# Attention scores of a unit in four column tiles of one PSUM bank, in a decode kernel on one core

## The chip, the cores and the metric

The kernel runs on one core of a Trainium2 chip. The metric is the device time of one execution in microseconds. A profiled execution has a span (first to last recorded event) and a time of its own that is a little longer; both are given below. The engines are called PE (matrix products), DVE (vector), ACT (activation), POOL and SP; PEld is PE's loading of the stationary operand. All large loads are started from SP's queue, in the order of the program.

## What is computed

One decode step for a batch of 2 and a model width D of 448. `xn` is the layer norm of `x`. There are 16 query heads over 8 key/value heads of width 256, and the window is the last 2048 of 8192 cached positions. All inputs are bf16.

```python
xn = layernorm(A_x)                                  # (2, 1, 448)
q  = (xn @ wq).reshape(2, 1, 16, 256)                # two query heads share one kv head
k, v = k_cache[:, :, -2048:, :], v_cache[:, :, -2048:, :]
p  = softmax(q . k * 256 ** -0.5)                    # per head, over 2048 positions
s  = (p . v).reshape(2, 1, 4096) @ wo                # (2, 1, 448)
g  = silu(relu(xn @ w1) @ w2)                        # w1 448 x 1792, w2 1792 x 448
out = A_x + s * g
```

## The kernel before, in words

The work on keys and values is cut into four **units**, u = 0 to 3, each with four kv heads of one batch entry. A unit has one key load and one value load of 4 MB, each as 128 partitions of 64 positions x 256 numbers (`kv_src`). They go into three buffers `ub`, by the table `place` (L242). A load into a buffer in use waits for the last reader of what is in it (`freed`). SP issues the loads in program order, so a load that waits holds all later ones.

For each unit:

- `do_turn` (L251): four DVE transposes bring the keys, as 32-bit pairs, from `ub` into `kt`. They wait for the key load, and for the scores of the unit before, which read `kt`.
- `do_S` (L288): 36 PE matmuls write the scores into `sbk`, 128 x 2048 f32: four with the mask `amask`, then 32 that stream 512 columns of `kt` each. Every matmul uses all 128 columns of the array (stationary `qz`, 128 x 128). `amask` adds a large negative number where a query head and a key row don't belong together.
- `do_chain` (L302): DVE takes the maximum of each row of `sbk` (L303); PE turns the 128 maxima into a row (L305), DVE reduces it (L307), PE spreads it back to partitions, DVE copies it to `bias` (L311), ACT computes the exponentials into `e_sb` with their sums (L312), and DVE transposes `e_sb` in 32 x 32 blocks into `pt` (L315).
- `do_sum` (L318): PE adds the sums over partitions, DVE takes the reciprocal into `rs` (L321).
- `do_PV` (L323): 32 matmuls with a stationary operand of 128 x 32 from `pt` and 512 columns of the values, in four column tiles of the array (`tile_position`, 32 columns each) into `obk`.
- `do_o` (L333): DVE scales `obk` into `o_sb` (L335), four small PE products turn it, DVE writes `at_exp` (L345).

Around them stand `do_q` (the projection to `q`, in column tiles too), `do_H` and `do_F` (the two products with `w1` and `w2`), and the product with `wo`. `w1` and `w2` are loaded into the buffer of `v2` and wait for `do_PV(2)`. Every engine runs its instructions in the order in which the calls from L385 on write them down; across engines there are only semaphores. That order is: turn 0, q, S 0, chain 0, sum 0, turn 1, S 1, chain 1, sum 1, PV 0, o 0, turn 2, S 2, chain 2, sum 2, PV 1, o 1, turn 3, S 3, PV 2, o 2, chain 3, sum 3, PV 3, o 3, H, F, product with `wo`. Nearly all matmuls are recorded under line 230 (the helper `mm`), so they are told apart by their tiles.

Of the kernel before, what the change touches and what calls it, by code (L numbers as in the profile page):

```python
# [74 lines left out]
def bass_recurrent_scan__sliding_block_cached__dense_activation_relu__decode_kernel(  # L75
# [22 lines left out]
    NU = 4  # L98
# [9 lines left out]
    with es:  # L108
# [19 lines left out]
        gsum = named("gsum", [128, 128], F32)  # L128
        amask = named("amask", [128, 128], BF)
        x_sb = named("x_sb", [128, D], BF)  # L130
# [6 lines left out]
        q_n = named("q_n", [128, 2048], BF)  # L137
        qz = named("qz", [128, NU * 8 * 128], BF)
        h_n = named("h_n", [128, FC], BF)
# [8 lines left out]
        bias = named("bias", [128, 1], F32)  # L148
        e_sb = named("e_sb", [128, NT * 32], BF)
        ssum = named("ssum", [128, 1], F32)  # L150
        rs = named("rs", [128, NU], F32)
        pt = [named(f"pt{i}", [128, NT * 32], BF) for i in range(2)]
        o_sb = named("o_sb", [128, 512], BF)
# [5 lines left out]
        kt = named("kt", [128, UW], BF)  # L159
        W2O = SLOTS * FC  # L160
        assert W2O + 14 * D <= UW

        sbk = psum("sbk", [128, 2048], F32)
        obk = psum("obk", [128, 512], F32)
# [30 lines left out]
        p_one = pr.op(POOL, lambda e: e.memset(one_f[:, :], 1.0), [p_idf])  # L195
        p_mr = pr.op(POOL, lambda e: e.memset(mrow[0:1, :], 0.0))
        p_am = pr.op(POOL, lambda e: e.memset(amask[:, :], -BIG))
        p_qz = pr.op(POOL, lambda e: e.memset(qz[:, :], 0.0))  # L198
# [20 lines left out]
        def fold_op(e):  # L219
            with nc.allow_low_precision("zeros and ones"):  # L220
                return e.tensor_reduce(out=fold[:, :], in_=view(ident, 0, [[1, 32], [32, 4]]), axis=AX.X, op=ALU.add)
        v_fold = pr.op(DVE, fold_op)
        v_gs = pr.op(DVE, lambda e: e.tensor_copy(
            view(gsum, 0, [[16, 8], [2, 8], [1, 2]]), view(fold, 0, [[0, 8], [1, 8], [0, 2]])), [v_fold])
        v_am = pr.op(DVE, lambda e: e.tensor_scalar(
            out=view(amask, 0, [[32, 4], [2, 4], [1, 2]]), in0=view(ident, 0, [[0, 4], [1, 4], [0, 2]]),
            scalar1=-1.0, scalar2=BIG, op0=ALU.add, op1=ALU.mult), [p_am, p_id])

# [31 lines left out]
        def do_q():  # L260
            deps = [d_wq, v_xr, st["obz"]]
            for s in range(SLOTS):
                for i in range(4):
                    lo = s * HC + i * 512
                    o = pr.op(PE, mm(obk[32 * i:32 * i + 4, :], xr[:, 4 * s:4 * s + 4], wqo[:, lo:lo + 512],
                                     s == 0, s == SLOTS - 1, tile_position=(0, 32 * i)), deps)
                    deps = []
            st["q_mm"] = o
            a_z0 = st["obz"]
            v = pr.op(ACTE, lambda e: e.activation(  # L270
                view(q_n, 0, [[256, 8], [32, 4], [1, 32]]), view(obk, 0, [[64, 8], [0, 4], [2, 32]]),
                ACT.Copy, scale=SCALE), [o, a_z0])
            v2 = pr.op(DVE, lambda e: e.tensor_scalar(  # L273
                out=view(q_n, 128, [[256, 8], [32, 4], [1, 32]]), in0=view(obk, 1, [[64, 8], [0, 4], [2, 32]]),
                scalar1=SCALE, scalar2=None, op0=ALU.mult), [v])
            deps = [v, v2, st["mbk"]]
            for ch in range(2):
                for wp in range(8):
                    o = pr.op(PE, mm(view(mbk, 32 * wp + ch, [[2, 16]]),
                                     view(q_n, 128 * (8 * ch + wp), [[1, 128]]),  # L280
                                     view(ident, 0, [[2, 2], [1, 2], [32, 4]]), True, True), deps)
                    deps = []
            for Q in range(4):
                st["q"] = st["mbk"] = pr.op(ACTE, lambda e, Q=Q: e.activation(  # L284
                    view(qz, 32 * Q, [[1024, NU], [128, 8], [1, 8]], n=32, p0=32 * Q),
                    view(mbk, 0, [[8, NU], [32, 8], [1, 8]], n=32, p0=32 * Q), ACT.Copy), [o, p_qz])

        def do_S(u):  # L288
            deps = [st["q"], st.get(("exp", u - 1)), v_am] + [st["turn", u, g] for g in range(4)]
            for g in range(4):  # L290
                o = pr.op(PE, mm(view(sbk, 512 * g, [[1, 512]]), amask[:, :], view(ident, 0, [[0, 128], [1, 4]]),
                                 True), deps)
                deps = []
            for wp in range(8):
                for g in range(4):
                    o = pr.op(PE, mm(view(sbk, 512 * g, [[1, 512]]),
                                     view(qz, 1024 * u + 128 * wp, [[1, 128]]),
                                     view(kt, g * UW // 4 + 64 * (wp // 2) + wp % 2, [[256, 16], [2, 32]]),
                                     False, wp == 7), deps)
            st["S", u] = o  # L300

        def do_chain(u):  # L302
# [4 lines left out]
            v = pr.op(DVE, lambda e: e.tensor_reduce(  # L307
                out=view(mrow, 0, [[32, 4], [1, 8]], n=1), in_=view(mbk, 0, [[0, 4], [1, 8], [32, 4]], n=1),
                axis=AX.X, op=ALU.max, negate=True), [m, p_mr])
            m = pr.op(PE, mm(mbk_ap(128, 1), mrow[0:1, :], one_f[0:1, :], True, True), [v, p_one])  # L310
            v = st["mbk"] = pr.op(DVE, lambda e: e.tensor_copy(bias[:, :], mbk_ap(128, 1)), [m])  # L311
            a = st["exp", u] = pr.op(ACTE, lambda e: e.activation(  # L312
                e_sb[:, :], sbk[:, :], ACT.Exp, bias=bias[:, 0:1], accum_out=ssum[:, 0:1]),
                [v, st.get(("pt", u - 1)), st.get(("gs", u - 1))])
            st["pt", u] = pr.op(DVE, lambda e: e.transpose(  # L315
                view(pt[u % 2], 0, [[64, NT // 2], [1, 2], [2, 32]]), e_sb[:, :]), [a, st.get(("PV", u - 2))])

# [5 lines left out]
        def do_PV(u):  # L323
            v, p = ub[place[f"v{u}"]], pt[u % 2]
            deps = [dma_of[f"v{u}"], st["pt", u], st.get(("osb", u - 1)), st["q"]]
            for k in range(NT // 2):
                g = k % 4
                o = pr.op(PE, mm(obk[32 * g:32 * g + 32, :], view(p, 64 * k, [[1, 32]]),
                                 v[:, 512 * k:512 * k + 512], k < 4, k >= 28, tile_position=(0, 32 * g)), deps)
                deps = []  # L330
            st["PV", u] = freed[f"v{u}"] = o

        def do_o(u):  # L333
# [5 lines left out]
            for dblk in range(2):  # L339
                for ts in range(2):  # L340
                    o = pr.op(PE, mm(mbk_ap(136 + 8 * dblk, 8), o_sb[:, 256 * ts + 128 * dblk:256 * ts + 128 * dblk + 128],
                                     view(fold, ts, [[2, 8]]), dblk == 0 and ts == 0, ts == 1), deps)
                    deps = []
# [5 lines left out]

        w12 = ub[place["v2"]]  # L350

        def do_H():
            for u in range(2):
                deps = [st["w1"], st.get("h_n"), st["fbz"]]
                for s in range(SLOTS):
                    lo = s * FC + u * (FC // 2)
                    o = pr.op(PE, mm(fbk[0:4, 0:FC // 2], xr[:, 4 * s:4 * s + 4], w12[:, lo:lo + FC // 2],
                                     s == 0, s == SLOTS - 1), deps)
                    deps = []
# [10 lines left out]
        def do_F():  # L370
            deps = [st["w2"], st["hT"], st["fbz"]]
            for f in range(14):
                for i in range(4):
                    lo = W2O + f * D + i * NCOL
                    o = pr.op(PE, mm(fbk[32 * i:32 * i + B, 0:NCOL], h_sb[:, 2 * f:2 * f + 2], w12[:, lo:lo + NCOL],
                                     f == 0, f == 13, tile_position=(0, 32 * i)), deps)
                    deps = []
# [13 lines left out]
        st["wbz"] = pr.op(ACTE, lambda e: e.memzero(wbk[:, :]))  # L391
        do_turn(0)
        do_q()
        do_S(0)
        do_chain(0)
        do_sum(0)
        load("k2")
        do_turn(1)
        load("v1")
        do_S(1)  # L400
        do_chain(1)
        do_sum(1)
        do_PV(0)
        do_o(0)
        load("k3")
        do_turn(2)
        load("v2")
        do_S(2)
        do_chain(2)
        do_sum(2)  # L410
        do_PV(1)
        do_o(1)
        load("v3")
        do_turn(3)
        do_S(3)
        do_PV(2)
        st["w1"] = pr.dma(SP, w12[:, 0:SLOTS * FC], w1_src, [freed["v2"]])
        st["w2"] = pr.dma(SP, w12[:, W2O:W2O + 14 * D].rearrange("p (hf f) -> p hf f", hf=2), w2_src, [freed["v2"]])
        d_wo = []
        j0 = 0  # L420
        for n in WO_PARTS:
            d_wo.append((j0, pr.dma(SP, wqo[:, j0 * D:(j0 + n) * D], wo_src[:, j0 * D:(j0 + n) * D], [st["q_mm"]])))
            j0 += n
        do_o(2)
        do_chain(3)
        do_sum(3)
        do_PV(3)
        do_o(3)
        for b in range(2):
# [3 lines left out]
                view(at2, b, [[2, 32]]), mbk_ap(256 + 32 * b, 32)), [m_at])  # L433
        do_H()
        do_F()
# [46 lines left out]
```

## Time and profile before

| what | value |
|---|---|
| median of 3 runs (lowest, highest) | 159.79 us (157.24, 160.32) |
| time of the profiled execution, and its span | 158.94 us, 157.5 us |
| busy PE / PEld / DVE / ACT | 71.7 / 30.1 / 70.2 / 15.2 us |
| moved by DMA | 44.19 MB, 281 GB/s over the span |
| start of S 0, S 1, S 2, S 3 | 29.69, 56.92, 87.25, 117.77 us |
| start of turn 0, 1, 2, 3 | 13.29, 48.01, 78.31, 108.83 us |

The time lies 1.44 us above the span; that is kept as it is when a sum is made. The starts, from the timeline, show the rhythm: from one unit's scores to the next unit's it takes 27.2, 30.3 and 30.5 us. Durations are of the one profiled execution; the three times beside it differ by up to 2%.

### The profile page before, as it was taken

The page shows a single profiled execution, that of the slowest core. Times are in us where ns is not written, and L with a number is a line of the kernel's source. Part 1 is how long each engine was busy: PE and PEld are TensorE (multiplying, and loading weights), DVE is VectorE, ACT ScalarE, POOL GpSimd, SP SyncE. Part 2 cuts the span into 40 slices and gives each one's busy share as a digit, 9 for nine tenths or more (in the row PEclk, how much of TensorE's full clock was granted, in tenths as well). Part 3 has the DMA queues.
Part 4 walks back from the last instruction along what each step waited for, and adds up shares of the span by engine and source line. Part 5 has one row for each costly group of instructions (what it writes and reads, how often), then busy time and mean ns, then how long its engine had stood idle before and what let it go on. Part 6 is the DMA issues. An engine that isn't in the chain of part 4 may idle for free.

```text
span 157.5 us, 1293 instructions
## 1 busy us (share of the span) xinstructions
PE 71.7 (46%) x566; PEld 30.1 (19%) x566; DVE 70.2 (45%) x68; ACT 15.2 (10%) x20; POOL 5.2 (3%) x13
## 2 busy tenths in 40 slices
PE   0000043599210059924600898173009991346872
PEld 0000010234010013402100233030003440222252
DVE  2916963000649940064499101565980008252224
ACT  3300002700050000004000000220000000500000
POOL 7500000000000000000000000000000000000000
PEclk9999999999965556996555579955555899557699
DMA  4998999999996049930299899103992006999700
GB/s 134 466 466 350 466 441 474 400 400 458 474 400 271 0 133 400 400 133 0 67 391 449 333 416 424 50 4 133 400 416 117 0 0 207 416 434 409 287 1 5
DMA packets 2473, 44.19 MB, mean 281 GB/s; under 512 B 290, under 2 KB 548, under 8 KB 932
## 3 DMA queue, kind: packets, MB, share of 16 engines
q1 hardware_dynamic: 2440, 44.11, 67.2%
q8 instruction: 4, 0.07, 0.2%
q10 hardware_dynamic: 28, 0.00, 0.0%
q14 instruction: 1, 0.01, 0.0%
HBM read 44.11 MB, written 0.00 MB: 280 GB/s over the span
## 4 chain that ended last, share of the span: by engine, by line
PE 44%; DVE 32%; DMA 13%; ACT 7%; issue 2%; SPq 0%; DVEq 0%
PE sbk L230 26%; DVE kt L256 17%; DMA wqo<-in_A_wq_dram 13%; PE obk L230 10%; DVE rm L303 6%; ACT e_sb L312 5%; PE fbk L230 4%; PE mbk L230 3%; DVE pt L315 3%; DVE o_sb L335 2%; ACT qz L284 1%; DVE h_n L360 1%; PE mbk L305 1%; DVE q_n L273 1%; DVE mrow L307 1%
## 5 line engine op out<-in xcount | busy, mean ns | idle before, releaser
L256 DVE STREAM_TRANSPOSE kt<-ub 128x2048 f32<-128x2048 f32 x16 | 35.5, 2278 | 4.9 <-DMA ub<-in_A_k_cache_dram 4.9
L230 PE MATMUL sbk<-kt,qz 128*128 128x512 bf16 x128 | 34.6, 434 | 0.0
L303 DVE TENSOR_REDUCE rm<-sbk 128x1 f32<-128x2048 f32 x4 | 9.2, 2289 | 33.4 <-PE sbk L230 33.4
L230 PE MATMUL sbk<-ident,amask 128*128 128x512 bf16 x16 | 7.6, 627 | 30.6 <-DVE kt L256 28.9
L230 PEld LDWEIGHTS sbk<-kt,qz 128*128 128x128 bf16 x128 | 14.0, 110 | 21.4 <-issue 10.4
L312 ACT ACTIVATE e_sb<-sbk,bias 128x2048 bf16<-128x2048 f32 x4 | 7.9, 1968 | 98.2 <-DVE bias L311 98.2
L315 DVE STREAM_TRANSPOSE pt<-e_sb 128x2048 bf16<-128x2048 bf16 x4 | 10.0, 2498 | 8.5 <-ACT e_sb L312 8.5
L230 PE MATMUL obk<-ub,pt 128*32 128x512 bf16 x128 | 12.7, 567 | 2.0 <-DVE rs L321 2.0
L335 DVE TENSOR_SCALAR o_sb<-obk,rs 128x512 bf16<-128x512 f32 x4 | 3.0, 751 | 19.4 <-PE obk L230 19.4
L230 PE MATMUL obk<-wqo,xr 128*4 128x512 bf16 x28 | 3.2, 625 | 14.3 <-DMA wqo<-in_A_wq_dram 14.3
L230 PEld LDWEIGHTS sbk<-ident,amask 128*128 128x128 bf16 x16 | 1.7, 131 | 33.1 <-DVE kt L256 29.2
L230 PE MATMUL mbk<-ssum,gsum 128*128 128x1 f32 x8 | 2.3, 362 | 9.4 <-ACT e_sb L312 9.4
L230 PEld LDWEIGHTS obk<-ub,pt 128*32 128x32 bf16 x128 | 4.2, 128 | 7.8 <-issue 7.1
L305 PE MATMUL mbk<-ident_f,rm 128*1 128x128 f32 x4 | 1.2, 296 | 9.7 <-DVE rm L303 9.7
L230 PE MATMUL fbk<-ub,xr 128*4 128x448 bf16 x14 | 4.2, 459 | 0.7 <-DVE h_n L360 0.7
L230 PEld LDWEIGHTS mbk<-ssum,gsum 128*128 128x128 f32 x8 | 2.0, 312 | 9.7 <-ACT e_sb L312 9.7
L230 PEld LDWEIGHTS obk<-wqo,xr 128*4 128x4 bf16 x28 | 0.8, 114 | 15.9 <-DMA wqo<-in_A_wq_dram 14.4
L230 PE MATMUL mbk<-ident,xg 2*128 2x2 bf16 x7 | 0.3, 163 | 7.2 <-DVE xg L207 7.2
L198 POOL MEMSET qz<- 128x4096 bf16 x1 | 3.5, 3507 | 0.0
L360 DVE TENSOR_SCALAR h_n<-fbk 4x448 bf16<-4x448 f32 x2 | 1.2, 612 | 4.1 <-PE fbk L230 4.1
L273 DVE TENSOR_SCALAR q_n<-obk 128x1024 bf16<-128x1024 f32 x1 | 1.2, 1225 | 3.9 <-ACT q_n L270 3.9
L270 ACT ACTIVATE q_n<-obk 128x1024 bf16<-128x1024 f32 x1 | 1.0, 1024 | 19.6 <-PE obk L230 19.6
(61 smaller groups left out, 34.6 us busy)
## 6 DMA issues: line engine op xcount, KB each, us to landing
ub<-in_A_k_cache_dram SPq DMA_DIRECT2D x4, 4096.0 KB, 21.0
ub<-in_A_v_cache_dram SPq DMA_DIRECT2D x4, 4096.0 KB, 13.6
wqo<-in_A_wq_dram SPq DMA_DIRECT2D x1, 3584.0 KB, 20.3
ub<-in_B_w_dram SPq DMA_DIRECT2D x2, 1568.0 KB, 8.3
wqo<-in_A_wo_dram SPq DMA_DIRECT2D x2, 1120.0 KB, 13.9
wqo<-in_A_wo_dram SPq DMA_DIRECT2D x1, 896.0 KB, 16.9
wqo<-in_A_wo_dram SPq DMA_DIRECT2D x2, 224.0 KB, 17.0
x_c<-in_A_x_dram ACTq DMA_DIRECT2D x2, 0.9 KB
```

Of the source, the lines that this page charges most:

```text
L198: p_qz = pr.op(POOL, lambda e: e.memset(qz[:, :], 0.0))
L230: return lambda e: e.matmul(out_ap, lhsT=lhsT, rhs=rhs, start=start, stop=stop, skip_group_check=True, **kw)
L256: st["turn", u, g] = pr.op(DVE, lambda e, lo=lo, hi=hi: e.transpose(k32[:, lo:hi], s32[:, lo:hi]), [dma_of[f"k{u}"], st.get(("S", u - 1))])
L273: v2 = pr.op(DVE, lambda e: e.tensor_scalar(out=view(q_n, 128, [[256, 8], [32, 4], [1, 32]]), in0=view(obk, 1, [[64, 8], [0, 4], [2, 32]]) ...
L284: st["q"] = st["mbk"] = pr.op(ACTE, lambda e, Q=Q: e.activation(view(qz, 32 * Q, [[1024, NU], [128, 8], [1, 8]], n=32, p0=32 * Q), view(mb ...
L303: v = pr.op(DVE, lambda e: e.tensor_reduce(out=rm[:, :], in_=sbk[:, :], axis=AX.X, op=ALU.max), [st["S", u]])
L305: m = pr.op(PE, lambda e: e.matmul(mbk_ap(0, 128, 1), lhsT=rm[:, :], rhs=ident_f[:, :], start=True, stop=True, is_transpose=True), [v, p_i ...
L307: v = pr.op(DVE, lambda e: e.tensor_reduce(out=view(mrow, 0, [[32, 4], [1, 8]], n=1), in_=view(mbk, 0, [[0, 4], [1, 8], [32, 4]], n=1), ax ...
L312: a = st["exp", u] = pr.op(ACTE, lambda e: e.activation(e_sb[:, :], sbk[:, :], ACT.Exp, bias=bias[:, 0:1], accum_out=ssum[:, 0:1]), [v, st ...
L315: st["pt", u] = pr.op(DVE, lambda e: e.transpose(view(pt[u % 2], 0, [[64, NT // 2], [1, 2], [2, 32]]), e_sb[:, :]), [a, st.get(("PV", u - ...
L335: st["osb", u] = pr.op(DVE, lambda e: e.tensor_scalar(out=o_sb[:, :], in0=obk[:, :], scalar1=rs[:, u:u + 1], scalar2=None, op0=ALU.mult), ...
L360: st["h_n"] = pr.op(DVE, lambda e, u=u: e.tensor_scalar(out=h_n[0:4, u * (FC // 2):(u + 1) * (FC // 2)], in0=fbk[0:4, 0:FC // 2], scalar1= ...
```

## The change

1. **Scores.** The four groups g of a unit no longer fill 2048 columns of `sbk`; each goes to 32 partitions of a `sbk` of 128 x 512, in its own column tile of PE. The stationary operand is 128 x 32 (`qz` and `amask` shrink to 32 columns). There are still 36 matmuls of 512 moving columns.
2. **Maximum, exponentials and transpose** run over 512 columns instead of 2048.
3. **P is turned and spread.** DVE transposes `e_sb` (512 wide) into a new `ptd`; 16 matmuls (32 columns of the identity as stationary, 128 moving columns, in four column tiles) spread it into a new PSUM tile `pbk`; ACT copies that to `pt`. `do_PV` takes 16 columns of `pt` as stationary operand instead of 32.
4. **Own buffers** `w1_sb` and `w2_sb`, so that their loads wait for no reader.
5. **Order.** PV 0 and o 0 stand between turn 1 and S 1; PV 1 directly behind S 2 and before chain 2; chain 3 and sum 3 before o 2; H between o 2 and PV 3. SP's order is k0, wq, k1, v0, k2, v1, k3, v2, w1, v3, w2, wo.

The diff, cut to its core:

```diff
-        qz = named("qz", [128, NU * 8 * 128], BF)
+        qz = named("qz", [128, NU * 8 * 32], BF)
+        fold8 = named("fold8", [128, 8], F32)
...
-        sbk = psum("sbk", [128, 2048], F32)
+        w1_sb = named("w1_sb", [128, SLOTS * FC], BF)
+        w2_sb = named("w2_sb", [128, 14 * D], BF)
+        sbk = psum("sbk", [128, 512], F32)
+        pbk = psum("pbk", [128, 512], F32)
...
         def do_S(u):
             deps = [st["q"], st.get(("exp", u - 1)), v_am] + [st["turn", u, g] for g in range(4)]
-            for g in range(4):
-                o = pr.op(PE, mm(view(sbk, 512 * g, [[1, 512]]), amask[:, :], view(ident, 0, [[0, 128], [1, 4]]),
-                                 True), deps)
-                deps = []
-            for wp in range(8):
+            for wp in range(-1, 8):
                 for g in range(4):
-                    o = pr.op(PE, mm(view(sbk, 512 * g, [[1, 512]]),
-                                     view(qz, 1024 * u + 128 * wp, [[1, 128]]),
-                                     view(kt, g * UW // 4 + 64 * (wp // 2) + wp % 2, [[256, 16], [2, 32]]),
-                                     False, wp == 7), deps)
+                    if wp < 0:
+                        lhsT, rhs = amask[:, :], view(ident, 0, [[0, 128], [1, 4]])
+                    else:
+                        lhsT = view(qz, 256 * u + 32 * wp, [[1, 32]])
+                        rhs = view(kt, g * UW // 4 + 64 * (wp // 2) + wp % 2, [[256, 16], [2, 32]])
+                    o = pr.op(PE, mm(sbk[32 * g:32 * g + 32, :], lhsT, rhs, wp < 0, wp == 7,
+                                     tile_position=(0, 32 * g)), deps)
+                    deps = []
...
-            st["pt", u] = pr.op(DVE, lambda e: e.transpose(
-                view(pt[u % 2], 0, [[64, NT // 2], [1, 2], [2, 32]]), e_sb[:, :]), [a, st.get(("PV", u - 2))])
+            t = st["ptd", u] = pr.op(DVE, lambda e: e.transpose(ptd[:, :], e_sb[:, :]), [a, st.get(("sp", u - 1))])
+            deps = [t, st.get(("pt", u - 1))]
+            for g in range(4):
+                for Q in range(4):
+                    o = pr.op(PE, mm(pbk[32 * Q:32 * Q + 32, 128 * g:128 * g + 128], ident[:, 32 * g:32 * g + 32],
+                                     view(ptd, 8 * Q, [[32, 16], [1, 8]]), g == 0, True,
+                                     tile_position=(0, 32 * Q)), deps)
+                    deps = []
+            st["sp", u] = o
+            st["pt", u] = pr.op(ACTE, lambda e: e.activation(pt[u % 2][:, :], pbk[:, :], ACT.Copy),
+                                [o, st.get(("PV", u - 2))])
...
         do_turn(0)
+        load("k2")
         do_q()
...
-        load("k2")
         do_turn(1)
         load("v1")
+        do_PV(0)
+        load("k3")
+        do_o(0)
         do_S(1)
         do_chain(1)
         do_sum(1)
-        do_PV(0)
-        do_o(0)
-        load("k3")
         do_turn(2)
         load("v2")
+        st["w1"] = pr.dma(SP, w1_sb[:, :], w1_src)
         do_S(2)
+        do_PV(1)
+        load("v3")
         do_chain(2)
         do_sum(2)
-        do_PV(1)
         do_o(1)
-        load("v3")
-        do_turn(3)
-        do_S(3)
-        do_PV(2)
-        st["w1"] = pr.dma(SP, w12[:, 0:SLOTS * FC], w1_src, [freed["v2"]])
-        st["w2"] = pr.dma(SP, w12[:, W2O:W2O + 14 * D].rearrange("p (hf f) -> p hf f", hf=2), w2_src, [freed["v2"]])
+        st["w2"] = pr.dma(SP, w2_sb[:, :].rearrange("p (hf f) -> p hf f", hf=2), w2_src)
...
-        do_o(2)
+        do_turn(3)
+        do_S(3)
+        do_PV(2)
         do_chain(3)
         do_sum(3)
+        do_o(2)
+        do_H()
         do_PV(3)
...
-        do_H()
         do_F()
```

More of the change, by code (lines that the diff above doesn't have):

```diff
@@ L128, in bass_recurrent_scan__sliding_block_cached__dense_activation_relu__decode_kernel @@
         gsum = named("gsum", [128, 128], F32)
-        amask = named("amask", [128, 128], BF)
+        amask = named("amask", [128, 32], BF)
         x_sb = named("x_sb", [128, D], BF)
@@ L148, in bass_recurrent_scan__sliding_block_cached__dense_activation_relu__decode_kernel @@
         bias = named("bias", [128, 1], F32)
-        e_sb = named("e_sb", [128, NT * 32], BF)
+        e_sb = named("e_sb", [128, 512], BF)
+        ptd = named("ptd", [128, 512], BF)
         ssum = named("ssum", [128, 1], F32)
         rs = named("rs", [128, NU], F32)
-        pt = [named(f"pt{i}", [128, NT * 32], BF) for i in range(2)]
+        pt = [named(f"pt{i}", [128, 512], BF) for i in range(2)]
         o_sb = named("o_sb", [128, 512], BF)
@@ L159, in bass_recurrent_scan__sliding_block_cached__dense_activation_relu__decode_kernel @@
         kt = named("kt", [128, UW], BF)
-        W2O = SLOTS * FC
-        assert W2O + 14 * D <= UW
-        sbk = psum("sbk", [128, 2048], F32)
+        w1_sb = named("w1_sb", [128, SLOTS * FC], BF)
+        w2_sb = named("w2_sb", [128, 14 * D], BF)
+        sbk = psum("sbk", [128, 512], F32)
+        pbk = psum("pbk", [128, 512], F32)
         obk = psum("obk", [128, 512], F32)
@@ L195, in bass_recurrent_scan__sliding_block_cached__dense_activation_relu__decode_kernel @@
         p_one = pr.op(POOL, lambda e: e.memset(one_f[:, :], 1.0), [p_idf])
-        p_mr = pr.op(POOL, lambda e: e.memset(mrow[0:1, :], 0.0))
-        p_am = pr.op(POOL, lambda e: e.memset(amask[:, :], -BIG))
         p_qz = pr.op(POOL, lambda e: e.memset(qz[:, :], 0.0))
@@ L222, in bass_recurrent_scan__sliding_block_cached__dense_activation_relu__decode_kernel @@
         v_fold = pr.op(DVE, fold_op)
+        v_fold8 = pr.op(DVE, lambda e: e.tensor_reduce(
+            out=fold8[:, :], in_=view(ident, 0, [[1, 8], [8, 16]]), axis=AX.X, op=ALU.add), [p_id])
         v_gs = pr.op(DVE, lambda e: e.tensor_copy(
-            view(gsum, 0, [[16, 8], [2, 8], [1, 2]]), view(fold, 0, [[0, 8], [1, 8], [0, 2]])), [v_fold])
+            view(gsum, 0, [[8, 16], [1, 8]]), view(fold8, 0, [[0, 16], [1, 8]])), [v_fold8])
         v_am = pr.op(DVE, lambda e: e.tensor_scalar(
-            out=view(amask, 0, [[32, 4], [2, 4], [1, 2]]), in0=view(ident, 0, [[0, 4], [1, 4], [0, 2]]),
-            scalar1=-1.0, scalar2=BIG, op0=ALU.add, op1=ALU.mult), [p_am, p_id])
+            out=view(amask, 0, [[8, 4], [2, 4], [1, 2]]), in0=view(ident, 0, [[0, 4], [1, 4], [0, 2]]),
+            scalar1=-1.0, scalar2=BIG, op0=ALU.add, op1=ALU.mult), [p_id])
         def mm(out_ap, lhsT, rhs, start, stop=False, **kw):
@@ L284, in do_q @@
                 st["q"] = st["mbk"] = pr.op(ACTE, lambda e, Q=Q: e.activation(
-                    view(qz, 32 * Q, [[1024, NU], [128, 8], [1, 8]], n=32, p0=32 * Q),
+                    view(qz, 8 * Q, [[256, NU], [32, 8], [1, 8]], n=32, p0=32 * Q),
                     view(mbk, 0, [[8, NU], [32, 8], [1, 8]], n=32, p0=32 * Q), ACT.Copy), [o, p_qz])
@@ L307, in do_chain @@
             v = pr.op(DVE, lambda e: e.tensor_reduce(
-                out=view(mrow, 0, [[32, 4], [1, 8]], n=1), in_=view(mbk, 0, [[0, 4], [1, 8], [32, 4]], n=1),
-                axis=AX.X, op=ALU.max, negate=True), [m, p_mr])
+                out=view(mrow, 0, [[8, 16], [1, 8]], n=1), in_=view(mbk, 0, [[0, 16], [1, 8], [8, 16]], n=1),
+                axis=AX.X, op=ALU.max, negate=True), [m])
             m = pr.op(PE, mm(mbk_ap(128, 1), mrow[0:1, :], one_f[0:1, :], True, True), [v, p_one])
@@ L313, in do_chain @@
                 e_sb[:, :], sbk[:, :], ACT.Exp, bias=bias[:, 0:1], accum_out=ssum[:, 0:1]),
-                [v, st.get(("pt", u - 1)), st.get(("gs", u - 1))])
-            st["pt", u] = pr.op(DVE, lambda e: e.transpose(
-                view(pt[u % 2], 0, [[64, NT // 2], [1, 2], [2, 32]]), e_sb[:, :]), [a, st.get(("PV", u - 2))])
+                [v, st.get(("ptd", u - 1)), st.get(("gs", u - 1))])
+            t = st["ptd", u] = pr.op(DVE, lambda e: e.transpose(ptd[:, :], e_sb[:, :]), [a, st.get(("sp", u - 1))])
[9 more added lines that the diff above has]
+                                [o, st.get(("PV", u - 2))])
         def do_sum(u):
@@ L327, in do_PV @@
                 g = k % 4
-                o = pr.op(PE, mm(obk[32 * g:32 * g + 32, :], view(p, 64 * k, [[1, 32]]),
+                o = pr.op(PE, mm(obk[32 * g:32 * g + 16, :], view(p, 16 * k, [[1, 16]]),
                                  v[:, 512 * k:512 * k + 512], k < 4, k >= 28, tile_position=(0, 32 * g)), deps)
@@ L341, in do_o @@
                     o = pr.op(PE, mm(mbk_ap(136 + 8 * dblk, 8), o_sb[:, 256 * ts + 128 * dblk:256 * ts + 128 * dblk + 128],
-                                     view(fold, ts, [[2, 8]]), dblk == 0 and ts == 0, ts == 1), deps)
+                                     fold[:, 8 * ts:8 * ts + 8], dblk == 0 and ts == 0, ts == 1), deps)
                     deps = []
@@ L348, in do_o @@
                 in1=view(qmask, 0, [[0, 8], [0, 2], [1, 4]]), op=ALU.mult), [o, v_qm])
-        w12 = ub[place["v2"]]
         def do_H():
@@ L356, in do_H @@
                     lo = s * FC + u * (FC // 2)
-                    o = pr.op(PE, mm(fbk[0:4, 0:FC // 2], xr[:, 4 * s:4 * s + 4], w12[:, lo:lo + FC // 2],
+                    o = pr.op(PE, mm(fbk[0:4, 0:FC // 2], xr[:, 4 * s:4 * s + 4], w1_sb[:, lo:lo + FC // 2],
                                      s == 0, s == SLOTS - 1), deps)
@@ L373, in do_F @@
                 for i in range(4):
-                    lo = W2O + f * D + i * NCOL
-                    o = pr.op(PE, mm(fbk[32 * i:32 * i + B, 0:NCOL], h_sb[:, 2 * f:2 * f + 2], w12[:, lo:lo + NCOL],
+                    lo = f * D + i * NCOL
+                    o = pr.op(PE, mm(fbk[32 * i:32 * i + B, 0:NCOL], h_sb[:, 2 * f:2 * f + 2], w2_sb[:, lo:lo + NCOL],
                                      f == 0, f == 13, tile_position=(0, 32 * i)), deps)
```

## The prediction, made before the changed kernel was run

> **What bounds the kernel now.** I read the chain that ended last first, because no engine is busy for even half of the span.
>
> ```profile
> PE 44%; DVE 32%; DMA 13%; ACT 7%; issue 2%; SPq 0%; DVEq 0%
> ```
>
> Of this, the 13% of DMA is one piece, the wait for wq up to 21.77 us. Behind it the chain, in order of time, goes through PE, DVE and ACT one after another. One period of it, unit 1 (start, duration, what):
>
> ```profile
> 48.09 8.79 DVE kt L256 x4
> 56.88 0.05 issue
> 56.92 10.23 PE sbk L230 x36
> 67.15 0.02 issue
> 67.18 2.30 DVE rm L303
> ...
> 70.77 2.07 ACT e_sb L312 x2
> 72.84 0.04 issue
> 72.89 0.59 PE mbk L230 x2
> 73.47 3.56 PE obk L230 x24
> 77.03 0.02 issue
> 77.06 0.76 DVE o_sb L335
> ```
>
> Nothing overlaps here: turn, scores, maximum, exponentials, values, output, and then the next turn. No load stands in the period. The loads have room:
>
> ```profile
> DMA  4998999999996049930299899103992006999700
> ```
>
> Each digit is a slice of 3.94 us. Up to slice 13 the loads are dense (they are started ahead), then they come in bursts with gaps, because each waits for a reader. So the kernel is bound by latency along three engines; shortening a piece of the chain shortens the span, until the loads are dense everywhere.
>
> The third view is the stretches of scores and values (window, its length, busy PE, PEld, DVE, ACT, POOL; then granted clock, DMA share, GB/s):
>
> ```profile
> 56.90:61.50 4.60, 4.58 (x11) 1.58 (x12) 0.00 (x0) 0.00 (x0) 0.00 (x0) 0.50 0.76 278
> 61.50:67.15 5.65, 5.64 (x26) 2.30 (x24) 0.00 (x0) 0.00 (x0) 0.00 (x0) 1.00 0.98 423
> 73.40:77.00 3.60, 3.60 (x33) 1.12 (x32) 2.03 (x2) 0.00 (x0) 0.00 (x0) 0.50 0.00 0
> 128.20:130.10 1.90, 1.90 (x33) 0.76 (x32) 0.00 (x0) 0.00 (x0) 0.00 (x0) 1.00 0.00 0
> ```
>
> Scores start at half clock, 11 matmuls in 4.6 us (427 ns each); then the clock is full and 24 weight loads follow in 5.10 us (213 ns each). The 32 matmuls of PV, of the same 512 columns but in four column tiles, take 3.6 us at half clock and 1.9 us at full: four run side by side (8 x 427 ns = 3.42 us, and 0.18 us of drain).
>
> **The parts, step by step.**
>
> *Scores, 36 matmuls in four column tiles.* From the PV row: 9 x 427 ns + 0.18 = 4.03 us, at half clock, since the faster stretch comes only after 4.6 to 5.1 us of work. Now 10.2 us: 6.2 us less per unit. No row shows a tiled matmul whose moving operand is read with a step, as `kt` is (every second bf16). Bounds: 4.03 us if the step costs nothing, as it does untiled (213 ns for 512 columns is the rate of PV too); 36 x 427 + 180 ns = 15.5 us if the tiles don't overlap and the clock stays at half. I take 4.03, because the step is free in the nearest row.
>
> The Trainium skill speaks more modestly here: "TensorE: Matmul & The Clock Gate", Part 3, gives 3.07 times for four row tiles and 2.38 for three column tiles of 512 columns, while PV's 32 x 427 ns = 13.7 us in 3.6 us is 3.8 times. At 3.07 a unit's scores would take 5.0 us, and the sum below would end 4 us later; I go by the row.
>
> *Maximum over 512.* Between L307 (128 numbers, 0.28) and L303 (2048, 2.29) a number costs 1.05 ns: 0.68 us, was 2.29. *Exponentials:* between L270 (1024, 1.02) and L312 (2048, 1.97) a column costs 0.92 ns: 0.55 us, 0.65 with the reading of the sums, was 2.07. *Transpose:* 2.46 x 512 / 2048 = 0.62, with some overhead 0.65 us, was 2.46; bounds 0.62 and 0.75 (L335, 512 wide).
>
> *Spread, new.* Four groups of four matmuls of 128 columns: 4 x 107 ns + 0.18 = 0.6 us. Lower bound 0.4 (full clock); upper bound 16 serial weight loads of 146 ns (the longest of PV's), 2.3 us. I take 0.6, as in PV such loads run under the matmuls. *Copy on ACT:* about 0.55 us (the three 512-wide fills of L389 to L391 take 0.53 to 0.57). The compiled list of the changed kernel has two activation-table loads, as before, so Copy between exponentials adds none. The copy runs beside the sum's matmuls (0.59) and is hidden for all units; without that cover it costs 0.55 each, at most, in unit 3 only.
>
> So from the end of the scores to the reciprocal, with the waits of 0.02 to 0.05 of the chain: 0.70 + 0.32 + 0.31 + 0.43 + 0.19 + 0.67 + 0.67 + 0.64 + 0.60 + 0.16, together with 0.02 ahead, **4.71 us** (before, 8.2). The turn of the next unit is behind the reciprocal on DVE and needs the scores' `kt`; it starts there.
>
> *Order, walked through:*
> - S 0 starts at 29.69 as now (wq's landing, do_q and its qz copies are of the same size; the smaller qz fill on POOL, 3.5 us before 6.2, was never late). S 0 ends 33.72, reciprocal 38.43, turn 1 (8.80) to 47.23. k1 is long there.
> - PV 0 runs under turn 1: v0 was issued at 2.78 and the longest landing takes 38.4, so 41.2, and 3.6 later is 44.8. But o 0 now stands on DVE behind turn 1 and on PE ahead of S 1: 0.79 + 0.33 = 1.12 on the path. S 1 48.35 to 52.38, reciprocal 57.09, turn 2 to 65.89.
> - S 2 65.94 to 69.97. PV 1 is ahead of the row turn L305 in PE's queue, so chain 2 waits: its maximum is ready at 70.7, PV 1 ends at 72.3 (0.6 to 1.1 us at half clock, the rest at full: 2.3). This costs 1.6 of the 3.56 that PV 1 now costs behind the exponentials. Then 3.99 to the reciprocal, 76.26, o 1 as now 1.34, turn 3 (8.85) 77.60 to 86.45.
> - S 3 to 90.53, PV 2 2.3 to 92.83, 3.99 to 96.82, o 2 1.12: 97.94.
> - H now sits between o 2 and PV 3 in PE's queue and holds it: 2.61 + 0.66 + 2.61 + 0.66 + 0.54 = 7.08 (the first seven took 1.57 at full clock; then 6.0). To 105.0. P of unit 3 is ready by 97, so PV 3 waits for H alone. PV 3 takes 1.9 or 3.6 by the clock; after some 5 us of products with gaps I take the middle, 2.7: 107.7.
> - o 3 and the two turns of `at`: 2.08 (143.60 to 145.68 now), 109.8; from F's start to the last sum 3.31 (152.15 to 155.46), 113.1; the output 2.04, span **115.1**. With 1.44: **116.6 us**. The median of the runs shown is 0.85 above the profiled time, within what the runs differ, so I add nothing.
>
> *The loads under it.* k2 ends in slice 12, near 49.6, as now. Then v1 (issued 47.2 behind turn 1) and k3 with it, v2 and w1 behind turn 2 (65.9), v3 behind PV 1 (72.3), w2 and wo behind it. At 420 GB/s a load of 4.19 MB takes 10.0: v1 59.6, k3 69.6, v2 79.6, w1 83.4, v3 93.4, w2 97.2, wo 105.9. Each is 8 us or more ahead of its reader (turn 3 at 77.6, PV 2 at 90.5, H at 97.9, PV 3 at 105, F at 109.8), wo about 5. So the loads are dense from 1 to 106 us and hidden, and little more could be won without them binding.
>
> **Rivals.**
> 1. *The loads bind.* For it: the dense queue above. k3 and v2 moved 8.39 MB from 77.05 to about 98.9 now, 384 GB/s with the start. At that rate the 27.9 MB behind v0 (41.2) end at 113.7; then the last products and sums, 0.9, and 2.04: 116.6, time 118.1. If v3 holds PV 3, to 122. Against it: slices at 449 and 474.
> 2. *Stepped reads at half rate in tiles.* Scores 0.43 + 8 x 854 ns + 0.18 = 7.4 us, 3.4 more, four times: 130. Against it: the untiled row.
> 3. *The tiles don't run side by side* but the clock rises as now: scores stay at 10.2, 6.2 more in four units: 141. The shorter maximum, exponentials and transpose, and the order, remain. Against it: PV and F in the same form.
> 4. *Slower than before.* Serial tiles and a clock that stays at half, because a quarter of the array counts as little work: 15.5 us a unit, 11.5 more, four times 46: 162.6. It decides from 15.4 us per unit on. For it: no tiled stretch now starts at half clock and lasts over 3.6 us, so none shows the clock rise. Against it: the overlap in PV holds at half clock as well.
>
> **How the numbers follow.** Forecast 0.74, rival 1 0.08, rival 2 0.10, rival 3 0.05, rival 4 0.03. Faster by over 2% (what a measurement of this kernel can tell from no change) 0.96, slower 0.03, within 0.01. The low end: the spread at 0.4 takes off 0.8 in four units, H with one half at full clock 1.1, PV 3 at 1.9 another 0.8, and 0.75 less per unit, if the clock rises inside the scores, 3.0: 111. The high end: the spread at 2.3 adds 1.7 in four units, 6.8; PV 3 at half clock 0.9; the transpose at 0.75 four times 0.1: 124.7, 125; rival 1 lies inside, and rivals 2 to 4, 0.18, outside.
>
> **What would show it.** Right: scores of 4 us per unit, L306 near 0.7, starts of S 1 to S 3 near 48, 66 and 86, DMA digits of 9 up to slice 36 of 40 in a span of 115, PE held by H before PV 3. Wrong: scores of 7 us or more; a turn, PV or F that waits for its load; 16 spread matmuls of over 1 us; PV 1 longer than 2.6, which would delay chain 2.

## The result, and the profile after

The changed kernel takes 125.97 us (median of 4 runs, 125.68 to 126.27), the kernel before 159.37. The ratio is 0.797 (95% interval 0.789 to 0.805): a gain of 33 us where 43 were forecast (159.37 - 116.6), and 1 us above the top of the range. Of some kernels below a run or more is over 1.5% slower than the fastest; the medians contain such runs, while the ratios and their intervals leave them out. The profiled execution has a span of 124.6 us against the 115.1 of the sum, so 9.5 us have to be found.

One period of the chain that ended last, unit 1, after the change (start, duration, what):

```profile
50.42 3.99 PE sbk L233 x35
54.41 0.02 issue
54.44 0.70 DVE rm L306
55.14 0.04 issue
55.18 0.28 PE mbk L308
55.47 0.02 issue
55.49 2.29 DVE mrow L310
...
58.43 0.79 ACT e_sb L315 x2
59.22 0.02 issue
59.24 0.72 DVE ptd L318
59.96 0.04 issue
60.00 0.62 PE pbk L233 x16
60.62 0.53 PE mbk L233 x2
61.15 0.02 issue
61.17 0.17 DVE rs L333
61.34 8.80 DVE kt L259 x4
```

The scores fell from 10.23 to 3.99 us and the maximum from 2.30 to 0.70, as forecast. But one line stands out: L310, the reduction of 128 maxima on one partition, was 0.29 us as L307 before, and is 2.29 now. The timeline of unit 1 before (start, duration), with the maximum over 2048 scores and this reduction:

```profile
67.18 2.29 DVE L303 TENSOR_REDUCE rm<-sbk 128x1 f32<-128x2048 f32 x1 [10.31 <-PE sbk L230]
69.83 0.28 DVE L307 TENSOR_REDUCE mrow<-mbk 1x32 f32<-1x128 f32 x1 [0.36 <-PE mbk L305]
```

The groups after (busy time, mean of one in ns, then idle time before) show why it grew:

```profile
L306 DVE TENSOR_REDUCE rm<-sbk 128x1 f32<-128x512 f32 x4 | 2.8, 692 | 18.0 <-PE sbk L233 18.0
L310 DVE TENSOR_REDUCE mrow<-mbk 1x128 f32<-1x2048 f32 x4 | 9.1, 2278 | 3.7 <-PE mbk L308 3.7
```

It reads 1 x 2048 numbers, as many per partition as the old maximum over 2048 scores, which took 2.29 us. The view that it reads, `[[0, 16], [1, 8], [8, 16]]` (pairs of step and count), takes the same 16 x 8 numbers 16 times, once for every copy of the 8 results that it writes. This view is part of the change, though the list of changes and the diff above leave it out; the first experiment shows the line.

The loads are dense (tenths of busy time in 40 slices of 3.1 us), and none ends a wait behind v0:

```profile
DMA  5797999989798998989899969989997999700000
```

At the end of the chain stands a second piece that no step of the sum had:

```profile
118.29 0.79 PE fbk L233 x56
119.08 1.23 PE wbk L233 x100
120.31 1.14 issue
121.45 0.54 PE wbk L233 x28
```

("issue" is time in which the engine waited for nothing that the profile shows.) Before, the 128 matmuls with `wo` ran without a stop, in 1.75 us:

```profile
152.83 1.75 PE L230 MATMUL wbk<-wqo,at 128*2 128x112 bf16 x128
```

### The profile page after: what moved, and what is told of

The parts are those of the page before. It is cut to its first block, busy times and chain, and to the rows that moved or that the text cites. A ratio compares the mean times of both kernels' runs of the same rounds, so it can differ in the third digit from the quotient of the medians.

```text
span 124.6 us, 1421 instructions
## 1 busy us (share of the span) xinstructions
PE 48.0 (39%) x630; PEld 20.5 (16%) x630; DVE 63.6 (51%) x69; ACT 12.5 (10%) x24; POOL 2.3 (2%) x11
## 4 chain that ended last, share of the span: by engine, by line
DVE 37%; PE 36%; DMA 16%; ACT 5%; issue 4%; SPq 1%
DVE kt L259 20%; DMA wqo<-in_A_wq_dram 16%; PE sbk L233 13%; PE obk L233 9%; DVE mrow L310 7%; PE fbk L233 5%; PE mbk L233 5%; ACT e_sb L315 3%; DVE ptd L318 2%; DVE o_sb L347 2%; PE pbk L233 2%; PE wbk L233 1%; ACT qz L287 1%; DVE rm L306 1%; DVE h_n L370 1%
## 5 line engine op out<-in xcount | busy, mean ns | idle before, releaser
L233 PE MATMUL sbk<-kt,qz 128*32 128x512 bf16 x128 | 14.0, 611 | 0.0
L233 PE MATMUL obk<-ub,pt 128*16 128x512 bf16 x128 | 11.6, 525 | 2.2 <-DMA ub<-in_A_v_cache_dram 2.2
L306 DVE TENSOR_REDUCE rm<-sbk 128x1 f32<-128x512 f32 x4 | 2.8, 692 | 18.0 <-PE sbk L233 18.0
L310 DVE TENSOR_REDUCE mrow<-mbk 1x128 f32<-1x2048 f32 x4 | 9.1, 2278 | 3.7 <-PE mbk L308 3.7
L233 PE MATMUL sbk<-ident,amask 128*32 128x512 bf16 x16 | 2.5, 608 | 19.8 <-DVE kt L259 18.2
L315 ACT ACTIVATE e_sb<-sbk,bias 128x512 bf16<-128x512 f32 x4 | 2.7, 687 | 61.9 <-DVE bias L314 61.9
L233 PEld LDWEIGHTS sbk<-kt,qz 128*32 128x32 bf16 x128 | 4.7, 140 | 7.6 <-issue 7.6
L233 PE MATMUL fbk<-w_sb,xr 128*4 128x448 bf16 x14 | 5.5, 571 | 0.7 <-DVE h_n L370 0.7
L233 PEld LDWEIGHTS obk<-ub,pt 128*16 128x16 bf16 x128 | 3.9, 112 | 8.2 <-issue 4.7
L318 DVE STREAM_TRANSPOSE ptd<-e_sb 128x512 bf16<-128x512 bf16 x4 | 2.8, 711 | 3.4 <-ACT e_sb L315 3.4
L233 PEld LDWEIGHTS mbk<-one_f,mrow 1*128 1x128 f32 x8 | 1.4, 213 | 10.2 <-DVE mrow L310 10.2
```

The source lines that it names most:

```text
L233: return lambda e: e.matmul(out_ap, lhsT=lhsT, rhs=rhs, start=start, stop=stop, skip_group_check=True, **kw)
L306: v = pr.op(DVE, lambda e: e.tensor_reduce(out=rm[:, :], in_=sbk[:, :], axis=AX.X, op=ALU.max), [st["S", u]])
L310: v = pr.op(DVE, lambda e: e.tensor_reduce(out=view(mrow, 0, [[8, 16], [1, 8]], n=1), in_=view(mbk, 0, [[0, 16], [1, 8], [8, 16]], n=1), a ...
L315: a = st["exp", u] = pr.op(ACTE, lambda e: e.activation(e_sb[:, :], sbk[:, :], ACT.Exp, bias=bias[:, 0:1], accum_out=ssum[:, 0:1]), [v, st ...
L318: t = st["ptd", u] = pr.op(DVE, lambda e: e.transpose(ptd[:, :], e_sb[:, :]), [a, st.get(("sp", u - 1))])
```

## The experiments

### The row reduction reads each number once

The line that adds the tile `mr8` is left out here.

```diff
             v = pr.op(DVE, lambda e: e.tensor_reduce(
-                out=view(mrow, 0, [[8, 16], [1, 8]], n=1), in_=view(mbk, 0, [[0, 16], [1, 8], [8, 16]], n=1),
+                out=mr8[0:1, :], in_=view(mbk, 0, [[1, 8], [8, 16]], n=1),
                 axis=AX.X, op=ALU.max, negate=True), [m])
+            v = pr.op(DVE, lambda e: e.tensor_copy(
+                view(mrow, 0, [[8, 16], [1, 8]], n=1), view(mr8, 0, [[0, 16], [1, 8]], n=1)), [v])
```

> The changed kernel, but the maximum over the 16 partitions of a row is taken once per column (128 numbers read, 8 written), and a 128-wide copy spreads the 8 numbers. Theory A (the new L310 reads 16 x 8 x 16 = 2048 numbers where the old one read 128, and takes 2.28 us instead of 0.28; it is on the path in all four units): 2.28 goes, 0.28 + 0.02 + about 0.18 for the copy comes, 1.8 less in four units, 7.2: about 118.8 us. Rival (the loads bind once the path is shorter, the last wo part lands near 110.5): less than half of it, 122 us or more, with a wait for wo or v3 in the chain.

Measured: 117.53 us (116.56 to 118.51), ratio to the kernel before 0.738 (0.731 to 0.745). In its timeline (start, duration), unit 0:

```profile
34.31 0.28 DVE L311 TENSOR_REDUCE mr<-mbk 1x8 f32<-1x128 f32 x1 [0.36 <-PE mbk L309]
34.62 0.21 DVE L314 COPY mrow<-mr 1x128 f32<-1x128 f32 x1
```

0.28 and 0.21 stand where 2.28 stood, 1.8 less in each unit. 8.4 us are gained where 7.2 were expected; the rest is within what the runs differ. No load appears in the chain behind wq, so the rival falls at this length of the path. With this one line mended, the sum of the prediction (116.6) is met within 1 us. That is partly luck: smaller misses of both signs are left, listed further down, and they cancel in part.

> e1_mrow once more, beside the two others: 117.5 us, each unit's row reduction and copy 0.5 us together, starts of S 1 to S 3 near 48, 64 and 85, PE stopping after the 100th matmul of the wo product.

The repetition gave 116.7 us (114.04 to 120.72), with the reduction and the copy at 0.28 and 0.21 again.

### The same reading put into the kernel before

```diff
-                out=view(mrow, 0, [[32, 4], [1, 8]], n=1), in_=view(mbk, 0, [[0, 4], [1, 8], [32, 4]], n=1),
-                axis=AX.X, op=ALU.max, negate=True), [m, p_mr])
+                out=view(mrow, 0, [[32, 4], [1, 8]], n=1), in_=view(mbk, 0, [[0, 4], [1, 8], [0, 16], [32, 4]], n=1),
+                axis=AX.XY, op=ALU.max, negate=True), [m, p_mr])
```

> The kernel before with one edit: the reduction L307 reads each of its 128 numbers 16 times (2048 numbers, the same maxima). Theory (the reduction costs by the numbers that it reads, about 1.04 ns each, on one partition as on 128, and is on the path in all four units): 2.28 instead of 0.28 us, 8.0 us in four units, about 166.9 us. Rival (it costs by its 16 x 8 outputs or by the layout of the changed kernel): 0.3 us as before, about 158.9.

Measured: 166.74 us (166.14 to 167.37), ratio 1.052 (1.043 to 1.062), 7.4 more than the 159.33 (157.46 to 160.49) beside it, where 8.0 were expected.

```profile
41.73 2.28 DVE L307 TENSOR_REDUCE mrow<-mbk 1x32 f32<-1x2048 f32 x1 [0.36 <-PE mbk L305]
```

With the old layout and only 32 results the reduction takes the same 2.28 us. The numbers read set its time, not the layout or the results written.

### The scores' matmuls, one tile after another

```diff
-            for wp in range(-1, 8):
-                for g in range(4):
+            for g in range(4):
+                for wp in range(-1, 8):
```

> The changed kernel with the 36 score matmuls in another order: the nine of one column tile directly after each other, then the next tile. Same matmuls, same operands. Theory (four matmuls overlap only where neighbours in the order go to different tiles): a unit's scores take 10.2 us if the clock rises after some 4.8 us as in the kernel before, about 6 more than now in four units, 150 us; if the clock stays at half because a quarter of the array counts as little work, 15.4 us and about 171 us. Rival (the order of issue does not matter): 4.06 us and 126 us.

Measured: 139.72 us (138.43 to 141.61). The profiled execution took 138.63 us, 12.6 more than that of the changed kernel (126.08). The theory, in both its cases, and the rival miss. Stretches of unit 0's scores, then all of unit 1's (columns as in the prediction: after the length the busy PE and PEld with counts, at the end clock, DMA share, GB/s):

```profile
29.80:32.60 2.80, 2.80 (x9) 0.99 (x11) 0.00 (x0) 1.22 (x1) 0.00 (x0) 0.50 0.95 410
32.60:36.60 4.00, 3.94 (x29) 1.61 (x25) 0.02 (x1) 0.00 (x0) 0.00 (x0) 1.00 0.91 393
53.50:60.30 6.80, 6.79 (x36) 2.57 (x35) 0.21 (x1) 0.00 (x0) 0.00 (x0) 0.78 0.94 386
```

The scores take 6.8 us instead of 4.0 interleaved and 10.2 untiled. At full clock 29 matmuls went by in 4.0 us, 138 ns each, less than the 213 ns that 512 columns take alone: tiles still overlap in part when nine neighbours share one. And the clock rose after 2.8 us of this tiled work; rival 4 of the prediction had it stay at half. By the two chains the interleaved order is worth 2.7, 2.9, 2.9 and 3.3 us in the four units, 11.8 together, and the stop at the end (see below) is 0.7 longer here: 12.5 of the 12.6 us between the two spans.

### Order and tiles apart

The first kernel is the changed one with the old order of calls, the second the old one with the new order (w2 left in the buffer of v2, since there is no room for both). This is the edit of the first, cut to its core:

```diff
         do_S(1)
         do_chain(1)
         do_sum(1)
+        do_PV(0)
+        do_o(0)
...
-        do_PV(1)
-        load("v3")
         do_chain(2)
         do_sum(2)
+        do_PV(1)
...
-        do_H()
         do_PV(3)
```

> The changed kernel with the calls in the order of the kernel before (w1 and w2 in their own buffers, but issued where they were issued before). If the path is a plain sum of its pieces: o 0 and o 1 with their PV stand between a chain and the next turn again (3.6 + 1.35 us each, twice), H and F at the end: about 132.8 us, 7 more than the changed kernel. If the order was worth nothing: 126.

> The kernel before with the order of calls of the changed kernel and w1 in its own buffer; scores, maximum, exponentials and transpose as before. w2 stays in the buffer of v2 (there is no room for both) and its load is issued behind PV 2. As a sum of pieces: PV 0 under turn 1, PV 1 at full clock behind S 2, H ahead of PV 3: about 151 us, 8 less than the kernel before. With e3 this splits the gain of 33 us between order and tiles. Rival (order and tiles are not additive, since PV 1 ahead of chain 2 costs less when its scores warm the clock): more than 10 less.

Measured: 132.3 us (131.44 to 132.68), as expected, and 153.39 (150.06 to 154.06), with 159.1 for the kernel before beside both. The runs of the second spread over 4 us. So the order is worth 6.3 on the tiled kernel and 5 to 9 on the old one; the narrow layout is worth 26.8 in the old order and 24 to 28 in the new one. Within this scatter the two add up, as pieces of one serial chain would, and the rival (more than 10 less by the order alone) is not met.

### Where PE stops before the last 28 matmuls

The stop comes after the 100th matmul with `wo` in the changed kernel (1.14 us), in the serial one (1.84), with the old order (1.33), and with the mended reduction (0.80, in the repetition 0.64): after the same matmul, although this product starts anywhere from 110.6 to 130.8 us. All have 630 matmuls, before there were 566. Two kernels add tiny matmuls early, while PE waits for wq; this is the edit of the second, the first has 64:

```diff
+        for s in range(24):
+            pr.op(PE, mm(pbk[:, 0:2], xg[0:B, 128:256], ident[0:B, 0:B], True, True))
```

> e1_mrow with 64 more matmuls of 2 columns on PE, written into an unused part of PSUM while PE waits for wq (7 to 21 us). In the changed kernel PE stands still for 1.14 us after the 100th of the 128 matmuls of the wo product, in e1 for 0.80 us after the same one, with all data there. Theory (PE waits for its own instructions, at a fixed place of the instruction stream): the stop moves 64 matmuls ahead, to after the 36th, and the time stays at about 117.5 us. Rival (the stop belongs to the data: the fifth part of wo, or the clock): it stays after the 100th.

> e1_mrow with 24 instead of 64 additional matmuls of two columns early on PE. With none PE stops after the 100th matmul of the wo product, with 64 it does not stop there at all. Theory (PE waits for its own instructions, at a place of the stream that is fixed): a stop of about 1 us after the 76th, 117.5 us. Rival (the stop needs the stream to be at one certain length): none, 116.

With 64 more: 116.01 us (114.93 to 120.06), and no stop; neither the theory (after the 36th) nor its rival (after the 100th) had that. With 24 more: 117.41 us (115.91 to 119.57), and the stop is after the 76th, 24 matmuls earlier, as the theory had it. The timelines of PE, first with 64, then with 24:

```profile
107.54 3.27 PE L234 MATMUL wbk<-wqo,at 128*2 128x112 bf16 x128
```

```profile
110.90 1.61 PE L234 MATMUL wbk<-wqo,at 128*2 128x112 bf16 x76
112.77 1.38 PE L234 MATMUL wbk<-wqo,at 128*2 128x112 bf16 x52 [0.26 <-issue]
```

So the place goes with PE's own stream, not with the data. In the changed kernel's queues one packet of the instruction queue (0.02 MB) lies between 118 and 120 us, just ahead of the stop at 120.31. That PE waits for it fits the place but was not shown, nor why the stop is missing with 64. Its length goes with the pace in part: 1.1 to 1.8 us where the first 100 matmuls took 1.40 us, 0.6 to 0.8 where they took 2.2, but 0.26 with 24 more, at nearly that pace. The times of the runs can't price it, since 116.01 lies within the runs of the mended kernel; in the traces it is 0.3 to 1.8 us.

### Two further versions

Both are built on the mended reduction; the edits are cut to a few lines. The first moves `o_sb` and what follows for units 0 to 2 into the next unit's chain; the second also puts H under turn 3 (its maximum and copy on ACT), loads w1 ahead of v2, and puts F directly behind PV 3.

```diff
                 [v, st.get(("ptd", u - 1)), st.get(("gs", u - 1))])
+            if u > 0:
+                do_osb(u - 1)
+                do_oT(u - 1)
...
         do_turn(3)
+        do_H()
```

> e1_mrow with the scaling of the values' output (o_sb) and what follows it moved for units 0, 1 and 2 into the next unit's chain: o_sb while ACT computes the exponentials, its four products ahead of the spread, at_exp behind the transpose. If the path is the sum of pieces: 1.1 goes ahead of S 1, 1.3 ahead of turn 3, 1.1 ahead of H, some 0.3 comes back in each chain: about 2.6 less, 115 us. Rival (the loads bind): a load's landing appears in the chain and less than 1 us is won.

> e6_oslot with H under turn 3 (its maximum with zero and its copy on ACT instead of DVE), w1 loaded ahead of v2, and F directly behind PV 3. As a sum of pieces 7.4 us of H and about 0.5 of F go: 107 us. But the loads, dense from 1 us on, ended near 103 us in e1: if they bind, the last wo product waits for its part of wo, and the time is about 103 + 0.9 + 2.0 + 1.4, 108 us, with DMA at the end of the chain.

Measured: 114.02 us (113.52 to 114.55), ratio 0.719 (0.714 to 0.725), and 113.15 (112.6 to 113.94), ratio 0.715 (0.708 to 0.723). The first gains 3.5 us on the mended kernel where 2.6 were expected. In its profiled execution H and PV 3 took 6.1 and 1.9 us, against 7.4 and 3.55 in the changed kernel, which was no part of the plan, and the last part of `wo` already holds PE, for 0.43 us. So the loads are reached here. The second takes 7 us of PE work off the path and gains 0.9, no more than the runs of either differ. Its timeline and the end of its chain:

```profile
102.13 0.66 PE L234 MATMUL wbk<-wqo,at 128*2 128x112 bf16 x40 [0.39 <-DVE ea L409]
104.75 1.10 PE L234 MATMUL wbk<-wqo,at 128*2 128x112 bf16 x40 [1.96 <-DMA wqo<-in_A_wo_dram]
106.98 1.51 PE L234 MATMUL wbk<-wqo,at 128*2 128x112 bf16 x48 [1.13 <-DMA wqo<-in_A_wo_dram]
```

```profile
74.77 33.32 DMA wqo<-in_A_wo_dram
108.09 0.04 issue
108.13 0.38 PE wbk L234 x8
```

The product with `wo` now waits three times for its weights, the last of which land at 108.1. The loads bind: 44 MB, dense from the start. My 108 us missed it because I took 103 us as their end in the mended kernel. That was wrong there too: 0.22 MB still moved between 105 and 106 us and 0.11 MB between 106 and 107.

## Why the prediction was wrong, point by point

**The step that failed** is the third term of the sum of 4.71 us, "0.31", for the row reduction. I took L307's duration for L310, without counting what the new view reads: 16 x 8 x 16 numbers instead of 4 x 8 x 4. It measured 2.31 with its wait, 2.0 more in each of four units, and each is on the path: 8.0 us of the 9.5. The row to size it from was in the profile before: L303, 2048 numbers, 2.29 us. The starts of S 1, S 2 and S 3 show it as it adds up: 2.1, 4.3 and 6.4 us later than forecast. The cause is shown by taking it out (8.4 us back) and by putting it into the kernel before (7.4 us on).

The other 1.5 us, by the chain; the rows give, behind PE, PEld, DVE, ACT and POOL, the granted clock of a stretch of unit 3's scores, of the rest of them with PV 2, and of PV 3:

```profile
92.90:95.70 2.80, 2.79 (x28) 1.05 (x32) 0.00 (x0) 0.00 (x0) 0.00 (x0) 0.50 0.88 378
95.70:98.10 2.40, 2.40 (x44) 1.03 (x36) 0.69 (x1) 0.00 (x0) 0.00 (x0) 1.00 1.02 423
112.60:116.20 3.60, 3.59 (x34) 0.98 (x32) 0.19 (x1) 0.00 (x0) 0.00 (x0) 0.50 0.00 0
```

- *Exponentials* 0.79 instead of 0.65 and *transpose* 0.72 instead of 0.65: 0.2 a unit, 0.8. A straight line through 1024 and 2048 columns of ACT was too steep: 687 ns at 512, not 550.
- *H and PV 3*: H took 7.4 (7.08 forecast), PV 3 3.55 (2.7, the middle of 1.9 and 3.6). The clock was back at half, 0.50 granted. 1.2 more.
- *The stop of PE* in the product with `wo`, about 1, was unknown.
- Given back: unit 3's scores and PV 2 took 3.55 and 1.73 instead of 4.03 and 2.3, as the clock rose from 0.50 to 1.00 within the scores, 1.1; o 0, o 1 and o 2 took 0.95, 1.24 and 0.97 instead of 1.12, 1.34 and 1.12, 0.4.

Together 8.0 + 0.8 + 1.2 + 1.0 - 1.5 is 9.5, as measured.

**What held.** Scores in tiles with a stepped moving operand: 4.06, 3.99 and 4.03 us, against 4.03 forecast; the step of the operand adds nothing that shows, and rivals 2, 3 and 4 fall. In this case the interleaved tiles give 36 x 427 ns in 4.03 us, 3.8 times. An estimate from the 3.07 times that the Trainium skill ("TensorE: Matmul & The Clock Gate", Part 3) gives for four row tiles would have been 5.0 us; the measurement decides. The maximum (0.70), the spread (0.62), the copy hidden beside the sum's matmuls, PV 1 at 2.30 ahead of the row turn L308, and H holding PV 3 came as written.

**The loads.** In the changed kernel they were hidden as forecast: the last of them moved between 109 and 110 us, and the product with `wo` began at 118.9. Rival 1 was not the cause, but it stood close behind: 8 us of mended reduction still come out, the next 3.5 too, and then 7 us of moved work give 0.9.

The range missed since its high end was made of the costs that I had marked as unknown. An error in a term taken as known has no place in such a range.

## What to carry to other kernels

Price every view by the elements that the instruction reads, repeats with step 0 included: in these reductions 2048 numbers on one partition cost DVE 2.28 us, and on 128 partitions 2.29. When a layout changes, go through the small instructions of the chain again, not only through the large ones; reduce first, and spread the few results with a copy. In a serial chain four column tiles of one PSUM bank shorten what follows the scores as well (here the maximum from 2.30 to 0.70 us, the exponentials from 2.07 to 0.79), until the loads end the chain.

## What had not been expected of the hardware

- PE stopped for 0.3 to 1.8 us at a fixed place of its instruction stream, in a dense stretch of small matmuls; 24 matmuls added early moved the place by 24, with 64 there was no stop.
- Matmuls of one column tile directly after each other still overlap in part with the next tile's: 138 ns each at full clock, where one takes 213.
- The time to full clock is not fixed: 2.8 us of tiled work in the serial kernel's unit 0 and in the changed kernel's unit 3, while the 4.0 us of its units 1 and 2 stayed at 0.50, and 4.6 to 5.1 us of scores before. In unit 0 of the changed kernel the profile gives 1.00, but the 36 matmuls take 4.06 us, as at 0.50 in the other units; the granted clock can't be trusted there.
